# The first MLP split 6 and 10 instead of 8 and 8 around the attention, and two-source additions of 1e-9

## The chip, the core and the metric

The kernel runs on one core of a Trainium2 chip. A core has five engines with a queue of instructions each: TensorE (PE: matmuls, with PEld for the weight load ahead of each), VectorE (DVE), ScalarE (ACT), GpSimd (POOL) and SyncE (SP, which here issues nearly all DMAs). Each engine takes its own queue in order, and the engines wait for each other through semaphores. The metric is the device time of one execution in microseconds, the median of the runs.

## What is computed

Four batches of 576 positions go through block-causal attention with 8 heads of 64, then through two MLPs of 512 x 2048 x 512 on all 2304 rows, the second with a rational function instead of a squared ReLU.

```python
scores = scale * np.matmul(q, k.transpose(0, 1, 3, 2))
scores = np.where(block_i >= block_j, scores, -1000000000.0)   # blocks of 64
attn = np.exp(scores - np.max(scores, axis=-1, keepdims=True))
attn = attn / (np.sum(attn, axis=-1, keepdims=True) + 1e-09)
x = np.matmul(attn, v)                # 2304 x 512 after the heads are joined
h = np.maximum(x @ w_in, 0.0)         # first MLP, 2048 inner units
x = h * h @ w_out
h = x @ w_in2                         # second MLP
g = (a0 + a1*h + a2*h*h + a3*h*h*h) / (1 + |b0|*|h| + |b1|*h*h + 1e-6)
out = g @ w_out2
```

## The kernel before

Every MLP product is made three times with operands split into a high part in fp32r and the rest, `PAIRS`: high by high, low by high, high by low. The 2048 inner units of an MLP are 16 slices of 128. A slice has one tile of `w_in` (kind `i`) and one of `w_out` (kind `o`).

**The stages.** There are three.

- Attention with part A of the first MLP. The loop over `i` walks 128 slots; a slot is one group of score rows of one head (`GROUPS`). Heads 0 to 7 are visited twice with two slots each (slots 0 to 31), all later heads once with four slots. Heads below 10 (`PLAIN`) run in plain fp32, the others in split fp32r; slot 40 is the first of head 10. In slot `i` the scores of `i` are made (`emit_s`, PE), their maximum (`emit_max`, DVE, L342) and exponential (`emit_exp`, ACT, L355), the division of slot `i-1` is prepared (`emit_norm`, DVE and POOL; L367 and L378 add the 1e-9), and the transposes of slot `i-3` and the product with `v` of slot `i-4` follow on PE. Between them `advance` takes steps of `moe_a`, which is part A: 8 of the 16 slices, for one batch at a time, in two pieces of 320 and 256 columns (`SUBS`). A step is 3 matmuls. For each piece there is an h part (8 slices x 4 steps; each slice ends in `relu_square`, with two ACT operations, one on DVE, L526, and one on POOL, L527) and a y part (4 x 8 steps, with a copy by ACT each). Its sums go to DRAM (`yp`). `steps` sets how many steps a slot gets: one from slot 20 (`FIRST`) to 36 (`WIDE`), then as many that batch 0 ends at slot 68 (`SECOND`), then 4. Batches 0 to 2 run beside the attention; batch 3 runs behind it.
- Part B: the other 8 slices on all 2304 columns, in blocks of 384, 384, 512, 512 and 512 (`blocks2`), 40 units of 24 matmuls (lines 722 and 762), added to `yp`.
- The second MLP (part C) in blocks of 512, 512, 512, 384, 384, 80 units (lines 722 and 831).

**The weights** come packed and are converted on the chip by `Converter`: a 512 KB DMA into a raw buffer (3 buffers until part B, then 2), one ACT operation (L117), four DVE operations (L118, L119, L121, L122), and one call later the split, ACT (L110) and POOL (L111). `convA` converts the 16 tiles of part A in the attention, one call whenever `due(i)` steps up: at slots 3, 6, 9, 13, 16, 19, then 21, 23 and so on to 39, and 41. `convB` converts 12 tiles of part B beside batch 3's part A, one call per 9 steps, and the first three calls may move up to slot 64 (`gate_b`). `conv3`, one call per unit of part B, converts the rest of part B's tiles, then half of part C's into DRAM (`waiting`), then the other half. The tiles in `waiting` are loaded in B's last block and split by `split_late` (L714, L715), one per unit, into the first units of part C.

**Order.** The code above is the program's order, and a scheduler of the framework then sets the order in which each engine's queue holds the instructions.

## Time and profile before

| | us |
|---|---|
| median of 3 runs (1019.84 to 1020.8) | 1020.14 |
| the profiled execution | 1019.09 |
| its span, first to last instruction | 1016.9 |
| PE busy | 995.2 (98%) |
| PEld busy | 882.0 (87%) |
| DVE busy | 733.4 (72%) |
| ACT busy | 722.5 (71%) |
| POOL busy | 582.0 (57%) |

The profiled execution is 1.05 us under the median, and 2.2 us of it lie outside the span. A matmul's recorded duration overlaps that of the next, so PE counts as busy also where its matmuls are spaced out; the spacing of starts tells more. PEld is idle where matmuls come slowly: its share is 53 to 75% in the first 100 us and close to 100% from 200 to 400 us. The granted clock is 1.000, the 2.4 GHz level, in the whole span.

### The profile page before, as it was taken

What the parts mean: (1) busy time and instruction counts of PE and PEld (TensorE: products, weight loads), DVE (VectorE), ACT (ScalarE), POOL (GpSimd) and SP (SyncE); (2) the same over time, 40 slices, a digit from 0 to 9 for tenths busy, and PEclk for the clock granted to TensorE, in tenths of its full rate; (3) what the DMA queues carried; (4) which work ended last, traced back from release to release, by engine and by line L of the source; (5) the groups of instructions that cost most, each with busy time, mean ns of one, the idle gap of its engine ahead of it and who ended that gap; (6) DMA issues with size and microseconds to landing.
All of it is one profiled execution on the core that took longest, in us unless ns stands there. A gap on an engine that the chain in (4) does not pass through costs nothing. (4 is left out here: it accounts for less than half of the span.)

```text
span 1016.9 us, 16852 instructions
## 1 busy us (share of the span) xinstructions
PE 995.2 (98%) x5721; PEld 882.0 (87%) x5721; DVE 733.4 (72%) x1344; ACT 722.5 (71%) x1526; POOL 582.0 (57%) x632
## 2 busy tenths in 40 slices
PE   7999998999999999999999999999999999999997
PEld 5677998999999999999888888887888888899996
DVE  6899588868767646776667756887766766777766
ACT  7779687768777746564555557887787776787775
POOL 4677686868676745530132448767556554655552
PEclk9999999999999999999999999999999999999999
DMA  9766335233332204557656572001101100100000
GB/s 284 243 198 213 120 99 154 90 120 110 116 93 81 72 31 148 176 197 253 227 166 199 182 239 81 1 1 42 43 1 32 42 1 1 56 18 1 32 1 31
DMA packets 63892, 106.57 MB, mean 105 GB/s; under 512 B 16064, under 2 KB 34496, under 8 KB 63808
## 3 DMA queue, kind: packets, MB, share of 16 engines
q1 hardware_dynamic: 63520, 105.34, 32.3%
q8 instruction: 45, 0.74, 0.3%
q14 instruction: 39, 0.32, 0.1%
q10 hardware_dynamic: 288, 0.16, 0.1%
HBM read 79.17 MB, written 23.07 MB: 101 GB/s over the span
## 5 line engine op out<-in xcount | busy, mean ns | idle before, releaser
L831 PE MATMUL yc<-w_co,gc 128*128 128x512 f32 x864 | 211.8, 391 | 3.1 <-ACT gc L791 3.1
L722 PE MATMUL hc<-xc,w_ci 128*128 128x512 f32 (+1 forms) x960 | 211.2, 368 | 0.0
L722 PEld LDWEIGHTS hc<-xc,w_ci 128*128 128x128 f32 x960 | 176.1, 188 | 26.3
L831 PEld LDWEIGHTS yc<-w_co,gc 128*128 128x128 f32 x864 | 161.1, 188 | 36.0 <-ACT gc L791 4.6
L792 POOL TENSOR_TENSOR gc<-t,gc 128x512 fp32r<-128x512 f32 (+1 forms) x78 | 104.7, 1349 | 126.5 <-issue 103.6
L497 PE MATMUL ha<-xt,w_ai 128*128 128x320 f32 (+1 forms) x768 | 121.5, 304 | 0.1
L510 PE MATMUL ya<-ga,w_ao 128*128 128x320 f32 (+1 forms) x768 | 116.8, 299 | 3.3 <-ACT r L523 1.3
L817 POOL TENSOR_TENSOR wq<-wq,ab 128x512 f32<-128x512 f32 (+1 forms) x78 | 96.3, 1234 | 28.7 <-ACT wq L815 28.5
L497 PEld LDWEIGHTS ha<-xt,w_ai 128*128 128x128 f32 x768 | 107.5, 189 | 4.7 <-issue 3.0
L510 PEld LDWEIGHTS ya<-ga,w_ao 128*128 128x128 f32 x768 | 106.4, 189 | 5.1 <-ACT r L523 1.5
L762 PE MATMUL yb<-gb,w_bo 128*128 128x512 f32 (+1 forms) x480 | 105.8, 368 | 0.1
L722 PE MATMUL hb<-xb,w_bi 128*128 128x512 f32 (+1 forms) x480 | 105.8, 368 | 0.1
L791 ACT ACTIVATE gc<-t 128x512 fp32r<-128x512 f32 (+1 forms) x80 | 47.1, 589 | 72.9 <-DVE t L800 72.9
L818 DVE TENSOR_TENSOR t<-hc,t 128x512 f32<-128x512 f32 (+1 forms) x80 | 51.0, 637 | 66.1 <-ACT t L816 66.1
L762 PEld LDWEIGHTS yb<-gb,w_bo 128*128 128x128 f32 x480 | 87.6, 188 | 12.0 <-issue 0.5
L722 PEld LDWEIGHTS hb<-xb,w_bi 128*128 128x128 f32 x480 | 87.4, 188 | 11.6 <-ACT yo L515 0.5
L383 POOL TENSOR_SCALAR p<-p,stat 64x64 f32<-64x64 f32 (+4 forms) x110 | 63.2, 575 | 50.8 <-DVE stat L379 14.6
L418 DVE TENSOR_TENSOR pt<-tp,pt 128x512 fp32r<-128x512 f32 (+3 forms) x110 | 59.2, 540 | 28.2 <-ACT pt L417 25.9
L798 DVE SCALAR_TENSOR_TENSOR wq<-wq,ab 128x512 f32<-128x512 f32 (+1 forms) x80 | 55.4, 692 | 33.5 <-ACT ab L797 23.0
L400 PE MATMUL tp<-ident,p 128*128 128x128 f32 x480 | 77.7, 278 | 0.4 <-DVE xp L453 0.2
L417 ACT ACTIVATE pt<-tp 128x512 fp32r<-128x512 f32 (+3 forms) x110 | 52.8, 481 | 27.2 <-PE tp L400 25.7
L800 DVE SCALAR_TENSOR_TENSOR t<-t,coef,ab 128x512 f32<-128x512 f32 (+1 forms) x80 | 66.9, 836 | 1.7
(137 smaller groups left out, 1987.7 us busy)
## 6 DMA issues: line engine op xcount, KB each, us to landing
kr<-in_k_dram SPq DMA_DIRECT2D x32, 288.0 KB, 3.6
raw_ci<-in_wi_dram SPq DMA_DIRECT2D x16, 512.0 KB, 4.2
raw_co<-in_wo_dram SPq DMA_DIRECT2D x16, 512.0 KB, 4.4
qr<-in_q_dram SPq DMA_DIRECT2D x24, 320.0 KB, 3.3
raw_ai<-in_wi_dram SPq DMA_DIRECT2D x8, 512.0 KB, 5.9
raw_ao<-in_wo_dram SPq DMA_DIRECT2D x8, 512.0 KB, 4.1
raw_bi<-in_wi_dram SPq DMA_DIRECT2D x8, 512.0 KB, 3.5
raw_bo<-in_wo_dram SPq DMA_DIRECT2D x8, 512.0 KB, 3.5
```

The lines of the kernel that those rows point to most:

```text
L383: nc.gpsimd.tensor_scalar(pv, pv, st[r:P, 6 + n:7 + n], 0.0, op0=ALU.mult, op1=ALU.add)
L400: nc.tensor.transpose(ps[:, at:at + P], ptile(slots[i][0], t)[:, P * c:P * (c + 1)], ident)
L418: nc.vector.tensor_tensor(low, src, f(high), op=ALU.subtract)
L497: nc.tensor.matmul(ps[:, 0:n], w[:, zw, P * kk:P * (kk + 1)], xt[:, zx, kk, first:end], start=i == 0, stop=i == 3 * KK - 1)
L510: nc.tensor.matmul(ps[:, 0:n], wA["o", m][:, zw, P * c:P * (c + 1)], gs[m][:, zg, 0:n], start=i == 0, stop=i == 3 * HALF - 1)
L722: nc.tensor.matmul(ps[:, 0:n], w[:, zw, P * kk:P * (kk + 1)], xt[:, zx, kk, 0:n], start=i == 0, stop=i == 3 * KK - 1)
L762: nc.tensor.matmul(acc[j, c][:, 0:n], wB["o", m][:, zw, P * c:P * (c + 1)], g[:, zg, 0:n], start=m == 0 and i == 0, stop=last and i == 2)
L792: (nc.vector if u - 2 >= len(units) - END else nc.gpsimd).tensor_tensor(g[:, 1, 0:n], t, f(g[:, 0, 0:n]), op=ALU.subtract)
L798: nc.vector.scalar_tensor_tensor(w, w, Q0, r, op0=ALU.add, op1=ALU.mult)
L800: nc.vector.scalar_tensor_tensor(t, t, a0, r, op0=ALU.add, op1=ALU.mult)
L817: (nc.vector if u >= len(units) - END else nc.gpsimd).tensor_tensor(w, w, ab, op=ALU.mult)
L831: last = nc.tensor.matmul(acc[j, c], g[:, zg, P * c:P * (c + 1)], w3["o", m][:, zw, :], start=m == 0 and i == 0, stop=m == NM - 1 and i == 2)
```

## The change

- Part A takes 6 slices (`MA`), part B 10 (`MB`). `STEPS`, the steps of a batch, goes from 128 to 96: 2.5 steps per slot from slot 36 to 68 instead of 3.5, then 3 instead of 4. Part B has 50 units instead of 40.
- `convA` has 12 tiles instead of 16, and `due` one rate of 0.33: calls at slots 3, 6, 9 and so on to 39.
- `convB` still converts 12 tiles, but one per 7 steps instead of 9. `conv3` has 8 tiles of part B instead of 4 in an order of its own, then 20 tiles for `waiting` instead of 16, then 12 instead of 16.
- The two additions of 1e-9 (L367, L378) become `scalar_tensor_tensor`: (x + 1e-9) max x, with x as both sources.

```diff
-HALF = NM // 2
+MA = 6
+MB = NM - MA
...
-                nc.vector.tensor_scalar(sm[:, 1, :, t0:t1], sm[:, 0, :, t0:t1], 1e-9, None, op0=ALU.add)
+                raw = sm[:, 0, :, t0:t1]
+                nc.vector.scalar_tensor_tensor(sm[:, 1, :, t0:t1], raw, 1e-9, raw, op0=ALU.add, op1=ALU.max)
...
-        nc.vector.tensor_scalar(st[:, 4:4 + n], st[:, 2:2 + n], 1e-9, None, op0=ALU.add)
+        nc.vector.scalar_tensor_tensor(st[:, 4:4 + n], st[:, 2:2 + n], 1e-9, st[:, 2:2 + n], op0=ALU.add, op1=ALU.max)
...
-            for m in range(HALF):
+            for m in range(MA):
...
-    R1, R2, RS = 0.3, 0.5, 20
+    RATE = 0.33
 
     def due(i):
-        return int(i * R1) if i < RS else int(RS * R1 + (i - RS) * R2)
+        return int(i * RATE)
...
-    STEPS = 16 * HALF
+    STEPS = 16 * MA
...
-        return int(STEPS + 4 * (x - SECOND))
+        return int(STEPS + (x - SECOND) * STEPS / PER_B)
...
-    jobsB = [(f"b{kind}{m}", src[HALF + m], w2, kind, wB, m, nc.gpsimd)
-             for m in range(HALF) for kind, src in (("i", wi1), ("o", wo1))]
+    orderB = [(kind, m) for m in range(NB // 2) for kind in "io"] + [
+        ("i", 6), ("i", 7), ("i", 8), ("o", 6), ("i", 9), ("o", 7), ("o", 8), ("o", 9)]
+    jobsB = [(f"b{kind}{m}", {"i": wi1, "o": wo1}[kind][MA + m], w2, kind, wB, m, nc.gpsimd) for kind, m in orderB]
...
-    SPLITS = (73, 80, 87, 94)
+    SPLITS = (55, 60, 65, 70)
...
-        if n % 9 == 0:
-            convB(*(gate_b if n < 27 else paced))
+        if n % 7 == 0:
+            convB(*(gate_b if n < 21 else paced))
...
-    late = [(kind, m) for m in range(HALF, NM) for kind in "io"]
+    late = [(kind, m) for m in range(MA, NM) for kind in "io"]
...
-    units = [(j, m) for j in range(len(blocks2)) for m in range(HALF)]
+    units = [(j, m) for j in range(len(blocks2)) for m in range(MB)]
...
-        if u < 3 or u in (4, 6) or u > 6:
+        if u != 5:
             conv3(*done)
```

The scheduler's order shows the change at three places. First DVE's queue in slots 25 to 28, before: `raw_ao` and `cv_ao` are conversions of a weight tile, `stat` maxima of the scores, `s_0_1` is of part A.

```order
L342 TENSOR_REDUCE stat_124<-sx_738 128x1
L118 TENSOR_SCALAR raw_ao_585<-raw_ao_585 128x512
L119 SCALAR_TENSOR_TENSOR raw_ao_585<-raw_ao_585 128x512
L342 TENSOR_REDUCE stat_125<-sy_765 128x1
L121 TENSOR_SCALAR cv_ao_757<-cv_ao_757 128x512
L122 SCALAR_TENSOR_TENSOR cv_ao_757<-cv_ao_757,raw_ao_585 128x512
L342 TENSOR_REDUCE stat_126<-sx_782 128x1
L118 TENSOR_SCALAR raw_ao_639<-raw_ao_639 128x512
L526 SCALAR_TENSOR_TENSOR s_0_1_818<-ha_0_1_733,r_0_1_817 128x320
L342 TENSOR_REDUCE stat_127<-sy_835 128x1
L119 SCALAR_TENSOR_TENSOR raw_ao_639<-raw_ao_639 128x512
```

The same place in DVE's queue now:

```order
L344 TENSOR_REDUCE stat_124<-sx_738 128x1
L123 TENSOR_SCALAR cv_ao_730<-cv_ao_730 128x512
L124 SCALAR_TENSOR_TENSOR cv_ao_730<-cv_ao_730,raw_ao_499 128x512
L344 TENSOR_REDUCE stat_125<-sy_754 128x1
L344 TENSOR_REDUCE stat_126<-sx_771 128x1
L120 TENSOR_SCALAR raw_ao_552<-raw_ao_552 128x512
L529 SCALAR_TENSOR_TENSOR s_0_1_807<-ha_0_1_722,r_0_1_806 128x320
L121 SCALAR_TENSOR_TENSOR raw_ao_552<-raw_ao_552 128x512
L370 SCALAR_TENSOR_TENSOR sums_139<-sums_139 128x2x2
```

Two maxima now follow each other without a conversion's operations between them, and the addition to the sums is the new form (L370).

Second PE's queue over some slots of the fp32r heads, before: `sy` and `sx` are scores, `tp` transposes, `pv` products with `v`, `ha` part A's h part.

```order
L321 MATMUL sy_2543<-kk_2311,qh_2310 128x448
L321 MATMUL sy_2543<-k_two_1116,q_two_1115 128x448
L497 MATMUL ha_0_2_2550<-xt_1315,w_ai_435 128x320 x12
L457 MATMUL pv_0_2506<-pt_1409,vs_2394 128x320
L457 MATMUL pv_0_2506<-pt_1409,vs_2394 128x256
L457 MATMUL pv_0_2506<-pt_1409,vs_2394 128x128
L400 MATMUL tp_0_2516<-ident,p_1_98 128x128 x4
```

And now:

```order
L323 MATMUL sy_2358<-kk_2148,qh_2147 128x448
L323 MATMUL sy_2358<-k_two_1078,q_two_1077 128x448
L500 MATMUL ha_0_1_2344<-xt_1240,w_ai_346 128x320 x6
L500 MATMUL ha_0_2_2390<-xt_1240,w_ai_420 128x320 x3
L460 MATMUL pv_0_2327<-pt_1325,vs_2225 128x320
L460 MATMUL pv_0_2327<-pt_1325,vs_2225 128x256
L460 MATMUL pv_0_2327<-pt_1325,vs_2225 128x128
```

A slot holds 9 matmuls of part A instead of 12.

Third ACT's queue at the end of batch 3's second h part, before: `w_bo`, `w_bi` and `cv` are conversions for part B, `r`, `ga` and `s` part A's `relu_square`.

```order
L110 ACTIVATE w_bo_5751<-cv_bo_5695 128x512
L117 ACTIVATE cv_bi_5754<-raw_bi_5598 128x512
L523 ACTIVATE r_1_5_5772<-ha_1_5_5747 128x256
L524 ACTIVATE ga_1_5_5771<-r_1_5_5772 128x256
L525 ACTIVATE s_1_5_5773<-r_1_5_5772 128x256
L523 ACTIVATE r_1_6_5794<-ha_1_6_5778 128x256
L524 ACTIVATE ga_1_6_5793<-r_1_6_5794 128x256
L525 ACTIVATE s_1_6_5795<-r_1_6_5794 128x256
L110 ACTIVATE w_bi_5807<-cv_bi_5754 128x512
```

And now, at the last slice (`ga_1_5`) and the y part behind it:

```order
L112 ACTIVATE w_bo_5242<-cv_bo_5195 128x512
L527 ACTIVATE ga_1_5_5281<-r_1_5_5282 128x256
L528 ACTIVATE s_1_5_5283<-r_1_5_5282 128x256
L663 ACTIVATE xb_5421<-xb_5421 128x384 x3
L112 ACTIVATE w_bi_5292<-cv_bi_5245 128x512
L119 ACTIVATE cv_bo_5295<-raw_bo_5158 128x512
L518 ACTIVATE yo_1_0_5318<-ya_1_0_5288 128x256
L112 ACTIVATE w_bo_5328<-cv_bo_5295 128x512
```

The same conversion (`w_bo`, the fourth `o` tile of part B) stood ahead of slice 5 of 8 and now stands ahead of slice 5 of 6, the last.

## Rows read from the trace of the kernel before

**Rows 1.** The page's busy times, us, share of the span, instructions.

```profile
PE 995.2 (98%) x5721; PEld 882.0 (87%) x5721; DVE 733.4 (72%) x1344; ACT 722.5 (71%) x1526; POOL 582.0 (57%) x632
```

**Rows 2.** Stretches: length, PE, PEld, DVE, ACT, POOL busy us (count), clock, DMA share, GB/s.

```profile
38.20:93.20 55.00, 54.54 (x338) 40.70 (x337) 51.91 (x86) 46.44 (x115) 35.38 (x43) 1.00 0.68 207
93.20:112.00 18.80, 17.54 (x121) 14.44 (x121) 13.43 (x30) 12.22 (x33) 15.99 (x20) 1.00 0.57 187
...
186.90:328.00 141.10, 141.10 (x1106) 140.69 (x1104) 101.84 (x280) 109.17 (x294) 103.78 (x148) 1.00 0.34 102
225.00:250.00 25.00, 25.00 (x210) 24.94 (x210) 20.85 (x56) 21.56 (x59) 20.66 (x30) 1.00 0.38 108
358.00:415.10 57.10, 55.05 (x411) 54.23 (x410) 35.99 (x47) 32.49 (x75) 35.18 (x34) 1.00 0.30 103
```

**Rows 3.** Timeline of PE, 38 to 98 us: start, us, instructions, count.

```profile
40.64 0.95 PE L497 MATMUL ha<-xt,w_ai 128*128 128x320 f32 x3
...
92.86 0.28 PE L321 MATMUL sy<-kk,qh 128*128 128x64 f32 x1
```

**Rows 4.** Timeline of DVE, 69 to 79 us: start, us, instructions, count.

```profile
72.23 1.24 DVE L367 TENSOR_SCALAR sums<-sums 128x4 f32<-128x4 f32 x1
73.50 0.18 DVE L368 RECIPROCAL sums<-sums 128x4 f32<-128x4 f32 x1
```

**Rows 5.** DVE by line, 38.2 to 93.2 us: count | busy us, mean ns | idle.

```profile
L121 DVE TENSOR_SCALAR cv_ao<-cv_ao 128x512 f32<-128x512 f32 x7 | 7.7, 1095 | 1.0 <-ACT cv_ao L117 1.0
L119 DVE SCALAR_TENSOR_TENSOR raw_ao<-raw_ao 128x512 uint32<-128x512 uint32 x7 | 6.3, 906 | 0.1
...
L122 DVE SCALAR_TENSOR_TENSOR cv_ao<-cv_ao,raw_ao 128x512 uint32<-128x512 uint32 x7 | 5.2, 749 | 0.2
L367 DVE TENSOR_SCALAR sums<-sums 128x4 f32<-128x4 f32 (+1 forms) x5 | 4.1, 813 | 0.0
...
L118 DVE TENSOR_SCALAR raw_ao<-raw_ao 128x512 uint32<-128x512 uint32 x7 | 3.1, 439 | 0.0
```

**Rows 6.** ACT by line in the same stretch.

```profile
L117 ACT ACTIVATE cv_ao<-raw_ao 128x512 f32<-128x512 f32 x7 | 4.7, 677 | 0.0
L110 ACT ACTIVATE w_ao<-cv_ao 128x512 fp32r<-128x512 f32 x6 | 3.8, 628 | 0.0
```

**Rows 7.** Timeline of PE, 374 to 430 us, with idle before and releaser.

```profile
374.94 14.24 PE L510 MATMUL ya<-ga,w_ao 128*128 128x320 f32 x96
389.02 11.68 PE L497 MATMUL ha<-xt,w_ai 128*128 128x256 f32 x96
400.54 1.96 PE L510 MATMUL ya<-ga,w_ao 128*128 128x256 f32 x15
403.83 1.89 PE L510 MATMUL ya<-ga,w_ao 128*128 128x256 f32 x11 [1.34 <-ACT r L523]
...
415.11 4.33 PE L722 MATMUL hb<-xb,w_bi 128*128 128x384 f32 x24
```

**Rows 8.** The chain that ended last, in order of time: start, us, what.

```profile
742.41 5.44 PE hc L722 x24
...
917.56 3.12 PE hc L722 x18
```

**Rows 9.** ACT by line, 186.9 to 328 us: part A's work.

```profile
L524 ACT ACTIVATE ga<-r 128x320 fp32r<-128x320 f32 (+1 forms) x25 | 11.3, 450 | 0.5
...
L523 ACT ACTIVATE r<-ha 128x320 f32<-128x320 f32 (+1 forms) x24 | 9.9, 413 | 6.6 <-PE ha L497 5.2 <-PE pv L457 0.9 <-PE sy L321 0.2
...
L515 ACT ACTIVATE yo<-ya 128x320 f32<-128x320 f32 (+1 forms) x12 | 5.0, 419 | 0.9 <-ACT p L355 0.9
```

**Rows 10.** Timeline of ACT behind the attention.

```profile
402.33 0.63 ACT L110 ACTIVATE w_bo<-cv_bo 128x512 fp32r<-128x512 f32 x1 [2.98 <-DVE cv_bo L122]
```

**Rows 11.** Timeline of DVE there: conversions of part B's weights.

```profile
378.41 0.68 DVE L122 SCALAR_TENSOR_TENSOR cv_bi<-cv_bi,raw_bi 128x512 uint32<-128x512 uint32 x1
...
382.71 1.21 DVE L118 TENSOR_SCALAR raw_bo<-raw_bo 128x512 uint32<-128x512 uint32 x1 [3.63 <-DMA raw_bo<-in_wo_dram]
...
417.91 0.69 DVE L122 SCALAR_TENSOR_TENSOR cv_bo<-cv_bo,raw_bo 128x512 uint32<-128x512 uint32 x1
```

**Rows 12.** Timeline of PE in part C, the longest wait there.

```profile
707.44 2.11 PE L831 MATMUL yc<-w_co,gc 128*128 128x512 f32 x8 [1.60 <-ACT gc L791]
```

More of the change, by code (lines that the diff above doesn't have):

```diff
@@ L64, in attention_moe_moe @@
     xs2 = dram.tile([P, KK, NT], F32, name="xs2")
-    waiting = dram.tile([NM, P, 512], F32, name="waiting")
+    waiting = dram.tile([2 * MB, P, 512], F32, name="waiting")
     ident = const.tile([P, P], F32, name="ident")
@@ L507, in moe_a @@
                 ps = bank(f"ya{b_}_{s}_{c}")
-                for i in range(3 * HALF):
+                for i in range(3 * MA):
                     m, (zw, zg) = i // 3, PAIRS[i % 3]
                     nc.tensor.matmul(ps[:, 0:n], wA["o", m][:, zw, P * c:P * (c + 1)], gs[m][:, zg, 0:n],
-                                     start=i == 0, stop=i == 3 * HALF - 1)
-                    if i % 3 == 2 and i < 3 * HALF - 1:
+                                     start=i == 0, stop=i == 3 * MA - 1)
+                    if i % 3 == 2 and i < 3 * MA - 1:
                         yield
@@ L538, in attention_moe_moe @@
         (f"a{kind}{m}", src[m], wpool, kind, wA, m, nc.gpsimd)
-        for kind, src in (("i", wi1), ("o", wo1)) for m in range(HALF)])
+        for kind, src in (("i", wi1), ("o", wo1)) for m in range(MA)])
     load_qk(units[0], nc.scalar)
@@ L752, in attention_moe_moe @@
             g = gs.pop(u - LAG)
-            last = m == HALF - 1
-            if m == HALF // 2:
+            last = m == MB - 1
+            if m == MB // 2:
                 for c in range(KK):
@@ L801, in attention_moe_moe @@
             gf[u - 1] = t
-        split_late(u + len(blocks2) * HALF + LAG - SPLIT_AT, done)
+        split_late(u + len(blocks2) * MB + LAG - SPLIT_AT, done)
         if u < len(units):
```

17 lines of the change are left out of this document (9 added, 8 removed).

## The prediction

> **What bounds the kernel now.** I read the page's busy times first, then the stretches, then the timelines of the stretches where an engine stands out. PE is busy 98% of the span [rows 1], but that alone says little, since recorded matmuls overlap; PEld shows where matmuls really follow each other. From 186.9 to 328 us, 12 heads of the attention, PEld is busy in 140.69 of 141.10 us, while DVE, ACT and POOL have 72 to 77% [rows 2]: PE bounds there, and DVE, ACT and POOL have room. It is the same in parts B and C, where whole units follow each other at 5.44 us per 24 matmuls [rows 8]. The early attention is different. From 38.2 us (slot 20, just ahead of part A's first matmuls at 40.64) to 93.2 us (slot 40, head 10's first scores at 92.86) [rows 3], PEld has 40.70 of 55.00 us, and DVE 51.91, which is 94% [rows 2]. So in these 55 us DVE is the bound, with ACT next (46.44), and PE's work there is partly free. In 93.2 to 112 us PEld still has only 77% [rows 2]. Behind the attention, where batch 3's part A runs beside the conversions, PE waits a few us for ACT [rows 7], which itself waits 2.98 us for a conversion on DVE [rows 10]. The frame of the sum is thus: work moved from a stretch where DVE is the bound to one where PE is the bound and DVE is free should pay; work of PE moved between stretches that PE bounds should not matter.
>
> **PE's work that moves.** Per slice and batch, part A makes 24 matmuls of 320 columns and 24 of 256. The starts give 14.08 us per 96 (389.02 less 374.94), 146.7 ns each, and 11.52 per 96 (400.54 less 389.02), 120.0 ns each [rows 7]. Two slices less in four batches: 8 x 24 x (146.7 + 120.0) = 51.2 us less. In part B a matmul of 512 columns takes 5.44/24 = 226.7 ns and one of 384 takes 3.12/18 = 173.3 ns [rows 8], taken from part C, whose shapes are the same. Two slices more: 2 x 24 x (3 x 226.7 + 2 x 173.3) = 49.3 us more. Four steps (12 matmuls, 1.8 us) of the 51.2 lie before slot 40, where PE isn't the bound, and count nothing. So 49.4 less and 49.3 more: **-0.1 us**. The split by itself gains nothing while PE bounds both places.
>
> **Conversions in slots 20 to 40.** Before, ten conversions fall here (three `ai`, seven `ao`), now six. One costs DVE 439 + 906 + 1095 + 749 ns = 3.19 us [rows 5] and ACT 677 + 628 = 1.31 us [rows 6]. Four less: DVE 51.9 - 12.8 = 39.1 us, ACT 46.4 - 5.2 = 41.2 us. ACT becomes the bound of the stretch. The lowest end is ACT without a gap, 41.2 us, a gain of 13.8. At the 94% that DVE reaches now it would be 43.7. But ACT's exponential waits for DVE's maximum and both would be loaded alike, so I take ACT at 89%, 46.5 us: **-8.5 us**. The other end is a stretch that gives back only a third of DVE's 12.8, -4. What hides the four conversions afterwards: part B, where conv3 makes them one per unit of 4.2 to 5.4 us against 3.2 us of DVE; if that cover were gone they would cost their 12.8 us there. In slots 40 to 46 (93.2 to 112 us) the backlog of DVE no longer reaches over: PEld's share there rises from 77% towards that of later slots, 4 us of open time of which I take **-1.5 us** (0 to -3). In slots 0 to 20 the count of conversions is the same, six; I take **-0.5 us** for the additions (0 to -1.5).
>
> **The additions.** In this stretch L367 takes 813 ns on average, five times [rows 5], once 1.24 us, and the reciprocal of the same tile right behind it 0.18 us [rows 4]. The new form isn't in the trace. From above it costs what the old one does, from below what the reciprocal does, so its five save 0 to 3.2 us of DVE. I take it near the reciprocal, as it is as small; but with ACT as the bound this adds nothing to the term above.
>
> **The attention with less filler, slots 40 to 132.** From slot 68 a slot has 9 matmuls of part A instead of 12. Per head (four slots) PE takes 141.1/12 = 11.76 us now, and 12 matmuls at 133.3 ns less, 10.16 us, if it stays the bound. ACT has 109.17/12 = 9.10 us per head [rows 2], less one slice's two operations (450 + 413 ns [rows 9]) every second head: 8.67, 85% of the new pace where it was 77%. In h parts of 256 columns it is tighter: ACT without part A has 9.10 - (11.3 + 9.9 + 5.0)/12 = 6.9 us per head [rows 9], plus three slices at 0.8 to 0.86, 9.4 us, against PE's 5.36 + 36 x 0.120 = 9.7 (5.36 being 11.76 less 48 x 133.3 ns): 97%. The busiest 25 us before had ACT at 86% [rows 2] with PE undisturbed. Five such and similar parts of about 20 us lie in slots 40 to 132. Nothing in the trace shows ACT above 90% for so long, so the cost is bounded by 0 and by 8 us (ACT limited to its 86%: 9.4/0.86 = 10.9 per head, 1.2 more than 9.7, in some seven heads). I take **+3 us**. POOL and DVE lose half a slice of part A per head as well and stay below ACT.
>
> **Behind the attention.** Batch 3's part A shrinks by 12.8 us (counted above), but the same 12 tiles are converted beside it. Ten of them were left when its y part began: L122 from 378.41 to 417.91, nine intervals of 4.39 us [rows 11]. DVE waits for raw tiles in it, 3.63 us once [rows 11]: with three raw buffers a load starts only when an older tile is converted. From the first y part to the end of batch 3, PE now needs 72 matmuls of 320 and 144 of 256 columns, 27.8 us, while the ten conversions need 10 x 3.2 = 32 us at DVE's price and 43.9 at the pace shown. What queues behind them: ACT's split of the fourth `o` tile, the sixth of the ten, now stands ahead of the last slice's `ga`, without which the last y part can't run through. The first tile was done 4.1 us into the y part (379.09 less 374.94), so the sixth comes at 4.1 + 5 x 3.2 = 20 to 4.1 + 5 x 4.39 = 26 us, and PE wants it after 72 x 0.1467 + 72 x 0.120 + 15 x 0.120 = 21 us. The same split was late before: the last y part lasted from 400.54 to 415.11, 14.6 us instead of 11.5, 1.34 of the 3.1 in one wait for ACT [rows 7, 10]. I take 5.6 us of waiting in place of 3.1, **+2.5 us**. From below it is 0. From above, if the ten tiles keep 4.39 us each, the last is split 43.7 us into the y part, ahead of part B's first unit on ACT, whose product follows 2.5 us later, at 46.2; PE would be there at 27.8 + 36 x 0.1733 = 34.0, 12.2 us late against 3.1: +9.1.
>
> **Part C.** Splitting of late tiles reaches unit 13 instead of 9, close to the block's end where PE waits up to 1.60 us [rows 12], 2.7 in all around 700 us: **+0.5 us** (-1 to +2).
>
> **Sum.** -0.1 - 8.5 - 1.5 - 0.5 + 3 + 2.5 + 0.5 = -4.6 us. The profiled execution has 1019.09, so 1014.5 by it; the median stood 1.05 above, so **1015.5 us**. About 0.2% (2 us) is what a measurement here tells from no change.
>
> **Rivals.**
> - *The attention starves* (the slower side). With a quarter less of part A in each slot, ACT can't keep its dependent chain (maximum, exponential, transposes' copies) going at the new pace. If it can be busy no more than 82%, a head takes 8.6/0.82 = 10.5 us instead of a mean of 9.9 over slots 40 to 132 (16 heads at 10.16, seven at 9.36 with 2.5 steps), 0.57 x 23 = 13.1 us in place of my 3: 1025.6 us. It decides from about 84%, where the 4.6 us are used up. For it: no row shows ACT above 86% over 25 us. Against it: at 86% PE had no gap at all. The Trainium skill, Perfetto Trace Analysis, section Optimization Strategy, advises interleaving regimes with different busiest engines; by it, taking PE work out of the attention would be a loss. The rows agree only as far as PE was never short of work from 187 to 328 us.
> - *Everything early is gained.* ACT runs without gaps in slots 20 to 40 (-13.8) and nothing starves or stalls anew: -0.1 - 13.8 - 1.5 - 0.5 + 0.5 = -15.4: 1004.7 us. For it: DVE did run at 94% and later without gaps, so a bound engine can. Against it: ACT's waits for maxima.
> - *The conversions behind the attention set the end.* +9.1 in place of +2.5: 1022.1 us, just no change. For it: the measured pace of 4.39 us. Against it: that pace was partly the nine steps between calls, some 3.6 us.
> - *The early stretch keeps its pace*, as its slots wait for each other (scores, maximum, exponential, one score bank each) and not for DVE's time: -1 in place of -8.5: 1023 us. Against it: DVE has next to no idle time there [rows 5]. In this case the change doesn't do what it says: work leaves the stretch and time doesn't.
>
> **How the numbers follow.** Forecast 0.50, everything early 0.17, conversions 0.13, starving 0.12, early pace kept 0.08. Faster by over 0.2% (under 1018.1): most of the forecast's (0.44) and all of the second, 0.61. Within 0.2%: 0.05 of the forecast, 0.08 of the conversions and 0.05 of the last two, 0.18. Slower: the rest, 0.21. Cases of the forecast alone lie from 1009 to 1021; leaving out 1 in 10 on either side of all cases, the range is 1006 to 1023.
>
> **What would show it.** Right: slots 20 to 40 in 46 us with DVE below 90%; a steady head in about 10.2 us with PEld still near 99%; part B 49 us longer without waits; a wait of some 6 us around the last y part of batch 3. Wrong: slots 20 to 40 at 50 us or more; PEld below 95% in the steady attention with PE's waits on ACT or POOL; a wait of PE at part B's first product; new waits in part C. L367's successor at 0.2 us or at 0.8 tells which bound of the additions holds.

## The result and the profile after

The changed kernel takes 1035.53 us (median, 1033.55 to 1036.38) against 1019.99 of the kernel before on the same chip: a ratio of 1.0148 (1.0135 to 1.016), 15.5 us slower. The prediction said 1015.5 (1006 to 1023) and faster. The profiled execution has 1034.79 us, its span 1033.0, and this is where the 16.1 us between the spans came from. The marks are the maximum on DVE of slots 20, 40, 68 and 124, then the first matmul of part B, the first of part C and the end. (The marks 38.2 and 93.2 of the prediction are the maxima of slots 19 and 39, so its slots 20 to 40 are one slot early; the stretch is as long, 55.0 us. By one mark in both kernels it reads as follows.)

| stretch | before | after | difference | PE's work by count of steps | left over |
|---|---|---|---|---|---|
| slots 0 to 20 | 41.24 | 40.43 | -0.81 | 0 | -0.8 |
| slots 20 to 40 | 55.01 | 51.41 | -3.60 | -1.8 (4 steps) | -1.8 |
| slots 40 to 68 | 80.83 | 72.73 | -8.10 | -11.2 (28 steps) | +3.1 |
| slots 68 to 124 | 163.02 | 146.58 | -16.44 | -22.4 (56 steps) | +6.0 |
| slot 124 to part B | 75.01 | 59.95 | -15.06 | -16.0 (40 steps) | +0.9 |
| part B | 195.54 | 253.41 | +57.87 | +49.3 | +8.6 |
| part C | 406.23 | 408.49 | +2.26 | 0 | +2.3 |

A step is 3 matmuls of 133.3 ns on average (146.7 in slots 20 to 40, where all have 320 columns). "Left over" is the difference less PE's work. The -0.8 of slots 0 to 20 says nothing: two later profiles with the same code there have 39.66 and 41.67 us. The rows behind the table, stretches of the trace: length, busy time and count of PE, PEld, DVE, ACT, POOL, granted clock, DMA share, GB/s. Before:

```profile
0.00:41.24 41.24, 35.03 (x176) 23.44 (x177) 28.57 (x77) 29.54 (x90) 23.75 (x61) 1.00 0.86 271
41.24:96.25 55.01, 54.55 (x337) 41.06 (x335) 52.53 (x85) 46.75 (x117) 37.52 (x46) 1.00 0.68 209
96.25:177.08 80.83, 77.11 (x602) 73.48 (x601) 61.38 (x161) 59.65 (x161) 56.07 (x79) 1.00 0.43 128
177.08:340.10 163.02, 161.65 (x1266) 160.86 (x1267) 120.33 (x328) 124.71 (x338) 120.08 (x171) 1.00 0.33 99
340.10:415.11 75.01, 72.96 (x561) 72.11 (x561) 46.41 (x75) 44.01 (x108) 46.86 (x51) 1.00 0.29 98
415.11:610.65 195.54, 195.27 (x951) 172.37 (x949) 130.71 (x203) 111.61 (x203) 61.12 (x44) 1.00 0.63 207
610.65:1016.88 406.23, 398.68 (x1837) 338.71 (x1835) 293.42 (x419) 306.24 (x515) 236.63 (x184) 1.00 0.07 23
```

And after:

```profile
0.00:40.43 40.43, 34.51 (x176) 23.21 (x177) 29.76 (x79) 29.67 (x90) 26.05 (x62) 1.00 0.89 283
40.43:91.84 51.41, 50.90 (x324) 39.45 (x323) 38.55 (x70) 42.00 (x107) 28.89 (x41) 1.00 0.60 181
91.84:164.57 72.73, 67.49 (x518) 62.52 (x518) 55.17 (x152) 55.57 (x153) 50.33 (x75) 1.00 0.46 136
164.57:311.15 146.58, 142.88 (x1105) 139.47 (x1104) 123.23 (x323) 120.11 (x325) 113.71 (x165) 1.00 0.38 112
311.15:371.10 59.95, 57.42 (x439) 56.31 (x438) 35.58 (x66) 38.02 (x93) 38.03 (x43) 1.00 0.34 109
371.10:624.51 253.41, 247.43 (x1191) 218.78 (x1189) 153.76 (x235) 132.28 (x245) 68.18 (x51) 0.99 0.54 180
624.51:1033.00 408.49, 400.16 (x1837) 339.89 (x1835) 295.10 (x418) 306.84 (x515) 238.77 (x185) 0.99 0.07 23
```

The page's busy times after, which answer to [rows 1]:

```profile
PE 1000.8 (97%) x5577; PEld 879.6 (85%) x5577; DVE 731.2 (71%) x1340; ACT 724.5 (70%) x1522; POOL 564.0 (55%) x616
```

They tell little: PE has 5.6 us more in 144 recorded matmuls less. In the stretches two things stand out. In slots 68 to 124 PEld falls from 98.7% of the stretch to 95.1%, and a head takes 10.47 us (146.58/14) where 10.04 would have been PE's (11.64 less 12 x 0.1333). And part B, where PE was busy in 195.27 of 195.54 us, now has 6 us in which it isn't, and a granted clock below 1.

Most of the loss in part B has one place. The chain that ended last, in order of time, around part B's first block (start, us, what):

```profile
369.96 3.81 DMA raw_bo<-in_wo_dram
...
373.80 0.70 DVE raw_bo L120
374.49 1.70 DVE cv_bo L124
...
376.21 0.02 ACT w_bo L112
...
376.75 0.39 ACT yo L518 x2
377.14 1.66 DMA yp<-yo
...
378.91 0.39 ACT yo L518
...
379.35 5.49 PE hb L726 x16
```

The same on ACT's timeline (start, us, instruction, count, idle before and its releaser):

```profile
371.02 0.37 ACT L518 ACTIVATE yo<-ya 128x256 f32<-128x256 f32 x1
376.21 0.63 ACT L112 ACTIVATE w_bo<-cv_bo 128x512 fp32r<-128x512 f32 x1 [4.83 <-DVE cv_bo L124]
```

ACT stands 4.83 us at the split of a converted tile (`w_bo`), and behind it in ACT's queue are the copies `yo` out of the last PSUM banks of part A. PE, which has run part B's first two units from 371.10, wants these banks for its third and waits 3.89 us. (The last of the copies also waits for its output buffer, behind a DMA of 1.66 us.) The tile itself is late by its whole line: its load could start only at 369.96, when an older tile of the three in flight was converted. And once PE had waited, it came back at half the clock. PE's stretches there:

```profile
375.40:379.30 3.90, 0.06 (x1) 0.00 (x0) 2.57 (x4) 2.12 (x6) 1.50 (x2) 0.90 0.19 67
379.30:384.60 5.30, 5.25 (x16) 5.25 (x17) 2.61 (x5) 4.47 (x10) 2.98 (x2) 0.50 0.67 220
```

Behind 3.9 us with one matmul the granted clock is 0.50, the 1.2 GHz level, for the next 16 matmuls. They take 5.28 us (379.35 to 384.63), 330 ns each instead of 173.3: 2.5 us on top of the 3.9. That is 6.4 of part B's 8.6 us. PE's longest waits behind the attention, whole rest of the run (waited for: us in total, times, longest):

```profile
PE hb L726 <- ACT yo L518: 3.9, 1, 3.9
PE yc L835 <- ACT gc L795: 3.7, 3, 2.2
PE yb L766 <- DVE yp L771: 2.1, 2, 1.1
```

The third, the additions of `yp` at a block's end, is most of the rest of part B; why PE waits there now isn't shown. The second is the wait of [rows 12], 3.1 us in all before. Behind its longest, 2.18 us where before had 1.60, the clock fell again. PE's timeline there, and a stretch as above:

```profile
720.04 7.24 PE L835 MATMUL yc<-w_co,gc 128*128 128x512 f32 x24 [2.18 <-ACT gc L795]
```

```profile
719.80:723.30 3.50, 3.26 (x8) 2.58 (x9) 3.39 (x5) 2.90 (x6) 3.04 (x2) 0.51 0.00 0
```

The next matmul starts at 727.12: 24 matmuls take 7.08 us, at 226.7 ns each they would take 5.44. With 0.6 us more of waiting these 1.6 us are nearly all of part C's 2.3.

### The profile page after: what moved, and what is told of

Its sections match the earlier page's. It is cut to its first block, busy times and chain, and to the rows that moved or that the text cites. A ratio compares the mean times of both kernels' runs of the same rounds, so it can differ in the third digit from the quotient of the medians.

```text
span 1033.0 us, 16566 instructions
## 1 busy us (share of the span) xinstructions
PE 1000.8 (97%) x5577; PEld 879.6 (85%) x5577; DVE 731.2 (71%) x1340; ACT 724.5 (70%) x1522; POOL 564.0 (55%) x616
## 4 chain that ended last, share of the span: by engine, by line
PE 73%; DVE 10%; ACT 6%; DMA 6%; POOL 3%; issue 2%; SPq 0%; ACTq 0%; DVEq 0%; POOLq 0%
PE yc L835 15%; PE hc L726 15%; PE yb L766 9%; PE hb L726 9%; PE ha L500 5%; PE ya L513 5%; PE tp L403 4%; PE pv L460 3%; PE sx L323 3%; PE sy L323 3%; DMA raw_ci<-in_wi_dram 2%; PE pv L447 2%; DMA raw_bo<-in_wo_dram 2%; DVE t L804 1%; DVE ab L803 1%
## 5 line engine op out<-in xcount | busy, mean ns | idle before, releaser
L726 PE MATMUL hb<-xb,w_bi 128*128 128x512 f32 (+1 forms) x600 | 134.3, 373 | 3.9 <-ACT yo L518 3.9
L766 PE MATMUL yb<-gb,w_bo 128*128 128x512 f32 (+1 forms) x600 | 132.2, 368 | 2.1 <-DVE yp L771 2.1
L726 PEld LDWEIGHTS hb<-xb,w_bi 128*128 128x128 f32 x600 | 111.6, 191 | 18.1 <-ACT yo L518 4.2
L766 PEld LDWEIGHTS yb<-gb,w_bo 128*128 128x128 f32 x600 | 109.9, 189 | 16.9 <-ACT sb L528 1.5
L500 PE MATMUL ha<-xt,w_ai 128*128 128x320 f32 (+1 forms) x576 | 94.3, 306 | 0.0
L513 PE MATMUL ya<-ga,w_ao 128*128 128x320 f32 (+1 forms) x576 | 88.0, 298 | 2.5 <-ACT ga L527 1.9
L500 PEld LDWEIGHTS ha<-xt,w_ai 128*128 128x128 f32 x576 | 81.5, 189 | 4.5 <-issue 3.0
L513 PEld LDWEIGHTS ya<-ga,w_ao 128*128 128x128 f32 x576 | 80.4, 189 | 3.5 <-ACT ga L527 2.3
L530 DVE TENSOR_TENSOR gb<-sb,gb 128x512 fp32r<-128x512 f32 (+1 forms) x50 | 33.5, 669 | 69.0 <-ACT sb L528 68.9
L664 POOL TENSOR_TENSOR xb<-xb 128x512 fp32r<-128x512 f32 (+1 forms) x20 | 26.4, 1334 | 87.6 <-ACT xb L663 87.6
```

Of the source, the lines that this page charges most:

```text
L500: nc.tensor.matmul(ps[:, 0:n], w[:, zw, P * kk:P * (kk + 1)], xt[:, zx, kk, first:end], start=i == 0, stop=i == 3 * KK - 1)
L513: nc.tensor.matmul(ps[:, 0:n], wA["o", m][:, zw, P * c:P * (c + 1)], gs[m][:, zg, 0:n], start=i == 0, stop=i == 3 * MA - 1)
L726: nc.tensor.matmul(ps[:, 0:n], w[:, zw, P * kk:P * (kk + 1)], xt[:, zx, kk, 0:n], start=i == 0, stop=i == 3 * KK - 1)
L766: nc.tensor.matmul(acc[j, c][:, 0:n], wB["o", m][:, zw, P * c:P * (c + 1)], g[:, zg, 0:n], start=m == 0 and i == 0, stop=last and i == 2)
```

## The experiments

**The additions alone, and everything but the additions.** The first run is the kernel before with the two-source form, the second the changed kernel with the old form.

```diff
-        nc.vector.tensor_scalar(st[:, 4:4 + n], st[:, 2:2 + n], 1e-9, None, op0=ALU.add)
+        nc.vector.scalar_tensor_tensor(st[:, 4:4 + n], st[:, 2:2 + n], 1e-9, st[:, 2:2 + n], op0=ALU.add, op1=ALU.max)
```

> The kernel before (8 and 8 slices) with only the two additions of 1e-9 in their two-source form. In the profile of after, 88 of the small additions in the fp32r heads take 25.5 us where the old form took 18.9, and the long ones end within 20 ns of the end of a POOL instruction. Theory ports (a two-source addition waits for POOL's running instruction and lengthens the chain exponential, addition, division on POOL, transposes): 2 to 6 us slower than before, lost in slots 40 to 124, where 243.8 us become 246 to 250. Theory filler (the attention of after lost its pace for want of part A's matmuls, the additions do nothing): within 1 us of before, the stretch within 1 us of 243.8.

> The changed kernel (6 and 10 slices) with the two additions of 1e-9 in their old one-source form. Theory ports: slots 40 to 124, 219.3 us in after, come down by 4 to 7 us towards the 210.2 that the removed matmuls alone would leave (243.8 less 33.6), and the whole run by as much, to 1028 to 1031. Theory filler: the stretch stays within 1 us of 219.3 and the run within 1 us of 1035.5.

Measured: 0.9995 (0.9981 to 1.0009) of before for the first, 1035.37 us and 1.0136 (1.0116 to 1.0156) for the second, against 1.0148 for the whole change. The additions are not why the change lost; the theory of the ports, as an explanation of the total, falls. The mechanism is there all the same. DVE by line (count | busy us, mean ns | idle before), the additions in the fp32r heads between slots 68 and 124, before, in the first run, after and in the second run:

```profile
L378 DVE TENSOR_SCALAR stat<-stat 128x1 f32<-128x1 f32 (+1 forms) x56 | 11.3, 203 | 2.4 <-ACT p L355 2.1
```

```profile
L378 DVE SCALAR_TENSOR_TENSOR stat<-stat 128x1 f32<-128x1 f32 (+1 forms) x56 | 21.2, 379 | 2.4 <-ACT p L355 2.1
```

```profile
L381 DVE SCALAR_TENSOR_TENSOR stat<-stat 128x1 f32<-128x1 f32 (+1 forms) x56 | 18.1, 323 | 4.8 <-ACT p L357 4.1
```

```profile
L381 DVE TENSOR_SCALAR stat<-stat 128x1 f32<-128x1 f32 (+1 forms) x57 | 10.5, 184 | 5.5 <-ACT p L357 4.8
```

The two-source form takes 140 to 180 ns more on average. Where PE has 12 matmuls of part A per slot this changed nothing (163.03 us in slots 68 to 124 against 163.02). Where it has 9, the old form made these slots 2.4 us shorter (144.21 against 146.58), while slots 40 to 68 were 1.2 us longer (73.88 against 72.73): 1.2 us less in both together, where the theory of the ports had 4 to 7. Slots 40 to 68, 68 to 124 and part B of the second run:

```profile
94.06:167.94 73.88, 68.05 (x520) 62.80 (x519) 55.13 (x153) 56.30 (x155) 51.12 (x75) 1.00 0.46 137
167.94:312.15 144.21, 141.55 (x1100) 139.08 (x1101) 114.92 (x322) 119.16 (x323) 112.86 (x164) 1.00 0.39 112
372.17:622.98 250.81, 246.13 (x1190) 217.58 (x1189) 154.42 (x235) 132.10 (x245) 68.00 (x51) 0.99 0.56 182
```

**The conversions behind the attention.** The changed kernel with 10 instead of 12 tiles converted ahead of part B, the other 10 in the order of their use.

```diff
-NB = 12
+NB = 10
...
-        ("i", 6), ("i", 7), ("i", 8), ("o", 6), ("i", 9), ("o", 7), ("o", 8), ("o", 9)]
+        ("i", 5), ("i", 6), ("o", 5), ("i", 7), ("o", 6), ("i", 8), ("o", 7), ("i", 9), ("o", 8), ("o", 9)]
...
-        if u != 5:
-            conv3(*done)
+        conv3(*done)
```

> The changed kernel with 10 instead of 12 tiles of part B converted ahead of part B, the other 10 one per unit in the order in which they fall due. In after the last of the 12 is split at 381.1 us, PE waits 3.9 us at part B's first block, and runs the next 16 matmuls in 5.3 us at a granted clock of 0.50. Theory conversions (what stands ahead of part B's first products is the chain of conversions behind the attention, 4.2 us each, that cannot be shorter than the stretch left for it): both go, 6 to 8 us faster, 1027.5 to 1029.5 us, granted clock 1.000 throughout. Rival (DVE is loaded anyway, the wait moves to the first units of part B whose tiles come later): no more than 2 us faster, with new waits of PE in 380 to 420 us.

Measured: 1029.4 us, 1.0082 (1.0058 to 1.0105), so 6.1 us less than after's 1035.53 and 6.0 less than the run above, which was on the same chip. Part B is 249.16 us, 4.25 less; its wait for `yp` is still there (2.2 us). PE's timeline at part B's first block:

```profile
370.43 4.36 PE L726 MATMUL hb<-xb,w_bi 128*128 128x384 f32 x24
375.65 2.71 PE L726 MATMUL hb<-xb,w_bi 128*128 128x384 f32 x14 [0.86 <-ACT yo L518]
378.20 2.24 PE L766 MATMUL yb<-gb,w_bo 128*128 128x384 f32 x12
```

The wait is 0.86 instead of 3.89 us, and the 14 matmuls behind it go at full clock (2.55 us to the next group, 182 ns each). The two tiles less were what stood ahead of part B. New waits in part B stay small (0.4 and 0.3 us), so the rival doesn't hold.

**Filling the slots again.** The changed kernel, with one matmul more in every step of batches 1 and 2.

```diff
-                    nc.tensor.matmul(ps[:, 0:n], w[:, zw, P * kk:P * (kk + 1)], xt[:, zx, kk, first:end],
-                                     start=i == 0, stop=i == 3 * KK - 1)
+                    for again in range(2 if i % 3 == 0 and b_ in (1, 2) else 1):
+                        nc.tensor.matmul(ps[:, 0:n], w[:, zw, P * kk:P * (kk + 1)], xt[:, zx, kk, first:end],
+                                         start=i + again == 0, stop=i == 3 * KK - 1)
```

and the same in the y part.

> The changed kernel, where in batches 1 and 2 each step of part A makes its first product twice, 4 matmuls instead of 3, so that a slot from 68 on has 12 matmuls of part A again, as in the kernel before (the output is then not the reference's). That is 56 x 3 x 133.3 ns = 22.4 us more of PE in slots 68 to 124, which took 146.6 us in after and 163.0 before. Theory filler (with 9 matmuls per slot PE waits for the dependent chain of the attention, which 12 cover): the added 22.4 us cost only 16 to 18, 162.5 to 164.5 us. Rival (after's attention is longer for another reason, such as the order in the queues or the two-source additions): the full 22 or more, 168.5 us or over.

Slots 68 to 124 of this run:

```profile
165.82:328.51 162.69, 162.21 (x1273) 161.47 (x1271) 125.44 (x323) 120.10 (x325) 117.11 (x166) 1.00 0.35 102
```

22.4 us of matmuls more cost 16.1 us (162.69 less 146.58), and PEld is back at 99%. So 6.3 us of the changed kernel's slots 68 to 124 are waits that three matmuls per slot had covered: the 6.0 us left over in the table. This kernel was executed once, and both it and the changed kernel have the two-source additions.

**The split in the middle.** 7 and 9 slices, with the old additions.

```diff
-MA = 6
+MA = 7
...
-    RATE = 0.33
+    RATE = 0.37
...
-        if n % 7 == 0:
+        if n % 8 == 0:
```

> The split in the middle, 7 slices of part A and 9 of part B, with one-source additions, 12 tiles converted ahead of part B, 14 by the attention at a rate of 0.37. Slots 68 to 124 have 10.5 matmuls of part A each. If what the change costs were spread evenly, the run would stand halfway between 1020 and 1035.4, at 1027.7. Theory filler and conversions (both are covers that run out): nearly all is lost in the second step, since the conversions behind the attention need some 43 us and are left 49 at 8 slices, 43 at 7 and 37 at 6: 1020 to 1024.5 us, no wait of over 2 us at part B's first block. Rival (each slice moved costs alike): 1026 us or more.

Measured: 1024.04 us, 1.0017 (0.9999 to 1.0035). Stretches, slots 40 to 68, 68 to 124 and part B:

```profile
97.41:175.45 78.04, 74.15 (x570) 69.06 (x568) 57.01 (x156) 58.45 (x159) 53.35 (x77) 1.00 0.43 127
175.45:328.85 153.40, 151.35 (x1184) 150.18 (x1185) 120.77 (x325) 123.03 (x331) 118.15 (x168) 1.00 0.36 105
...
396.37:615.59 219.22, 219.22 (x1071) 194.31 (x1069) 139.13 (x217) 123.97 (x226) 67.15 (x49) 1.00 0.59 196
```

The first slice moved loses 2.8 us in slots 40 to 68 (78.04 against 80.83 less 5.6), 1.6 in slots 68 to 124 (153.40 against 163.02 less 11.2) and nothing in part B, where PE is busy throughout. The 6 and 10 split with the same old additions loses 4.3, 3.6 and 6.0 us in these places (73.88, 144.21 and 250.81), so the second slice adds 1.5, 2.0 and 6.0. The attention's loss thus begins with the first slice; only the cover of the conversions behind it runs out between 7 and 6 slices. The other 2.4 us of the changed kernel's 6.0 in slots 68 to 124 come with the two-source additions.

**What sets slots 20 to 40.** Six kernels, all made from the kernel before. First, the conversions called from slot 20 on without three of their four DVE operations:

```diff
-                nc.scalar.activation(c, high.bitcast(F32), AF.Abs, scale=65536.0)
+                nc.scalar.activation(c, high.bitcast(F32), AF.Abs, scale=1e-9 if light else 65536.0)
...
-                nc.vector.scalar_tensor_tensor(
-                    low, high, 0x80000000, low, op0=ALU.bitwise_and, op1=ALU.bitwise_or)
+                if not light:
+                    nc.vector.scalar_tensor_tensor(
+                        low, high, 0x80000000, low, op0=ALU.bitwise_and, op1=ALU.bitwise_or)
...
+        convA.light = i >= 20
```

> The kernel before, where the ten conversions called from slot 20 on leave out three of their four DVE operations (906 + 1095 + 749 ns each; the output is then not the reference's). That takes 27.5 us of DVE's 52.6 out of slots 20 to 40. The prediction's frame (DVE bounds these slots): the stretch from the maximum of slot 20 to that of slot 40, 55.1 us, comes down to ACT's 46.8 or a little more, 47 to 49 us. Theory PE (plain fp32 matmuls are recorded twice, at 242 ns for 288 columns, longer than the weight load ahead of them, so PE is dense there though PEld has 75%): the stretch stays at 53 us or more.

```profile
42.12:98.28 56.16, 53.86 (x322) 40.17 (x321) 27.84 (x59) 45.57 (x114) 33.37 (x46) 0.97 0.68 208
```

DVE is busy in 27.84 instead of 52.53 us, and the stretch isn't shorter. The clock was 0.97 in this one: 3.4 us of it were at half the clock (90.83 to 94.24), which is worth 1.7, so some 54.5 without. DVE alone doesn't bound it. (This kernel and the last three of the six were executed once each: 1025.65, 1020.01, 1018.68 and 1017.86 us, against 1021.8, 1020.88, 1018.4 and 1018.4 for the kernel before on the same chips.) Next, part A begun at slot 36:

```diff
-    FIRST, WIDE, SECOND = PER_B // 2 + MOE_AT, PER_B + MOE_AT, 2 * PER_B + MOE_AT
+    FIRST, WIDE, SECOND = PER_B + MOE_AT, PER_B + MOE_AT, 2 * PER_B + MOE_AT
```

> The kernel before with part A begun at slot 36 instead of 20: the 16 steps (48 matmuls) of slots 20 to 36 move into slots 36 to 68, which get 4 steps each instead of 3.5. Theory PE (PE bounds slots 20 to 40, and slots 40 to 68 have waits that more of part A can fill): slots 20 to 40 lose 6 to 9 us, slots 40 to 68 gain 4 to 6, the run is 1 to 3 us faster. Theory of the prediction (DVE bounds slots 20 to 40, PE's work is free there): slots 20 to 40 keep 54 us or more, slots 40 to 68 gain 6.4, the run is 5 to 6 us slower.

Slots 20 to 40 and 40 to 68:

```profile
43.01:97.12 54.11, 48.81 (x294) 33.73 (x291) 51.94 (x85) 45.66 (x112) 35.73 (x44) 1.00 0.72 227
97.12:183.38 86.26, 83.06 (x646) 79.95 (x644) 63.71 (x162) 62.36 (x166) 58.82 (x81) 1.00 0.41 120
```

14 steps less (6.2 us of PE) shorten the first by 0.9 us only and lengthen the second by 5.4, nearly all of what they are. The run is slower, 1.0034 (1.0021 to 1.0048). The theory of PE, with 6 to 9 us, missed. By this run alone the prediction's theory would stand (54 us or more in the one, nearly all of the steps' time paid in the other; it had the run 5 to 6 us slower, and it was 3.5), but the run before it shows that relieving DVE alone gains nothing. Slots 40 to 68 have no room for more of part A. The same kernel with 10 tiles ahead of part B as well:

```diff
-NB = 12
+NB = 10
...
+    orderB = [(kind, m) for m in range(NB // 2) for kind in "io"] + [
+        ("i", 5), ("i", 6), ("o", 5), ("i", 7), ("o", 6), ("o", 7)]
...
-        if u < 3 or u in (4, 6) or u > 6:
+        if u < 6 or u > 6:
```

> The kernel before with part A begun at slot 36, as in the run above, and with 10 instead of 12 tiles of part B converted ahead of part B, the other six one per unit in the order in which they fall due. Theory conversions: the waits of 2.8 us in batch 3's last part and at part B's first block (one of 1.34 for ACT) shrink by 1 to 2 us, with no new ones in part B: 1 to 2 us faster than the run above. Rival (the waits there come from the y part's own chain): no difference to the run above beyond 0.5 us.

Measured 1.0069 (1.0053 to 1.0085): not faster, but slower still, so both theories missed. From slot 124 to part B it took 76.1 us against 74.7: the wait for ACT became 1.89 us (0.9 in the run above), with 3.4 us at half the clock behind it. Part C took 2.1 us more (408.14 against 406.00); why isn't shown. At 8 slices taking two conversions away from ahead of part B gains nothing.

Next, the conversions from slot 20 on without ACT as well as without the three DVE operations:

```diff
-                nc.scalar.activation(c, high.bitcast(F32), AF.Abs, scale=65536.0)
+                if light:
+                    nc.vector.tensor_scalar(c, high.bitcast(F32), 1e-9, 0.0, op0=ALU.mult, op1=ALU.add)
```

and the rounded copy likewise.

> The kernel before, where from slot 20 on the conversions for part A use ACT no more: their two ACT operations (677 + 628 ns) become two short ones on DVE, and three of DVE's four operations are left out as in the earlier run that did only that (the output is then not the reference's). DVE stays under 40 of 55 us, ACT loses some 13 of 46.8 us in slots 20 to 40. Theory ACT (ACT's queue, in order and with the exponentials' waits in it, sets the pace of these slots: 0.85 of the stretch in before, 0.82 in after, 0.84 where part A's steps were taken out, and 56.2 us where DVE alone was relieved): the stretch from 55.0 to 45 to 49 us. Rival (the slots wait for each other, scores, maximum, exponential, transposes, whatever the conversions do): 53 us or more.

```profile
42.22:97.63 55.41, 54.46 (x340) 41.93 (x339) 46.03 (x80) 37.15 (x99) 37.48 (x47) 1.00 0.74 228
```

ACT has 37.15 instead of 46.75 us (DVE 46.03, since its replacements were longer than thought), and the stretch stays. The theory of ACT falls. Last, no conversions at all from slot 20 on, with part A as before and with part A begun at slot 36:

```diff
-        for kind, src in (("i", wi1), ("o", wo1)) for m in range(HALF)])
+        for kind, src in (("i", wi1), ("o", wo1)) for m in range(HALF)][:6])
...
-    wA = {}
+    class Reused(dict):
+        def __missing__(self, key):
+            return self["i", 0]
+
+    wA = Reused()
```

> The kernel before without the ten conversions called from slot 20 on, altogether: no DMA of the packed tile, nothing on ACT, DVE or POOL; part A uses the first converted tile in place of the ten missing ones (the output is then not the reference's). Taking DVE's share of them away (56.2 us) or DVE's and ACT's (55.4) left the 55.0 us of slots 20 to 40 as they were. Theory conversions (their DMAs of 512 KB and POOL's subtractions of 1.4 us, which were still there in those two runs, hold the slots up, and that is what the change saved with four conversions less): 46 to 50 us. Rival (the slots wait for each other, whatever runs beside them): 52.5 us or more.

> The kernel before without these ten conversions and with part A begun at slot 36 instead of 20: slots 20 to 36 hold the attention alone (the output is then not the reference's). Part A's steps taken out alone gave 54.1 us. Rival (the slots wait for each other): 50 us or more with nothing beside them. Theory of shares (PE's work of part A and the conversions each hide behind the other, so that only taking both away shows): 42 to 47 us.

Slots 20 to 40 of the one and of the other:

```profile
40.67:93.83 53.16, 52.15 (x330) 40.65 (x329) 26.21 (x51) 37.83 (x99) 24.16 (x39) 1.00 0.48 142
```

```profile
40.46:87.22 46.76, 46.23 (x293) 34.32 (x291) 23.27 (x49) 35.98 (x94) 21.29 (x37) 1.00 0.53 150
```

Without conversions 53.16 us, without part A 54.11, without both 46.76. The theory of shares holds: two loads of nearly the same length lie over each other, and taking one away shows the other. With the conversions gone, PE counts one for one: 14 steps less give 6.4 us less (14 x 3 x 146.7 ns are 6.2). PE's own floor for these slots was 53.2 us, and PEld was busy in only 40.65 of them, 76%. The changed kernel has four steps less there, 1.8 us, and four conversions less: 53.16 less 1.76 is 51.40, and it took 51.41. (That it meets the floor so exactly is luck: at 7 slices, with two steps and three conversions less, the same sum gives 52.28, and it took 53.06.)

Which engine carries the second load isn't shown. With part A taken out DVE had 51.94 of 54.11 us, so it may well be DVE there. Nor is it shown what of the conversions holds the stretch 1.9 us above PE's floor: without ACT's work for them and with DVE at 46.03 us it was 55.41, with DVE at 27.84 some 54.5. And without any conversions the whole run was no faster (1018.68 against 1018.4), as slots 68 to 124 took 1.6 us more, with 3.4 us at half the clock at their start.

**A version that beats both.** The kernel before, where POOL instead of ACT makes the rounded copy of a converted tile of part A, and the same with 7 slices in part A (the edit of the split in the middle, with two rates of conversions).

```diff
-                nc.scalar.activation(w[:, 0, :], c, AF.Copy)
+                if nm[0] == "a":
+                    eng.tensor_scalar(w[:, 0, :], c, 1.0, 0.0, op0=ALU.mult, op1=ALU.add)
+                else:
+                    nc.scalar.activation(w[:, 0, :], c, AF.Copy)
```

and for the second also

```diff
-    RATE = 0.33
+    R1, R2, RS = 0.3, 0.42, 20
```

> The kernel before, where the rounded copy of a converted weight for part A (628 ns on ACT, 16 times) is made by POOL, which then subtracts it as before. ACT loses 6.3 us of its 46.8 in slots 20 to 40 and some 4 us ahead of them; POOL gains some 9 us of its 37.6. Theory ACT: slots 20 to 40 become 3 to 5 us shorter, and the run 3 to 6 us faster than before, 1014 to 1017.5. Rival (slots wait for each other, or POOL, whose divisions stand in the same chain, becomes late): within 1.5 us of before or slower.

> 7 slices in part A and 9 in part B with one-source additions, as in the run of the split in the middle, with the rounded copies on POOL as in the run above and conversions in the attention at a rate of 0.3 until slot 20 and 0.42 then. Theory ACT: two conversions less in slots 20 to 40 are worth some 2 us on top of the run above and the thinner attention costs 1.6 us in slots 68 to 124, so it stands level with the run above, within 2 us. Rival (a slice moved to part B costs anyway): 3 us or more slower than the run above, as the middle split was against before.

Measured: 0.9964 (0.995 to 0.9979) of before for the first, 1016.91 us; 0.9995 (0.9979 to 1.0011) for the second, 3.3 us slower than the first, as its rival said. Two conversions less were worth nothing in its slots 20 to 40: 55.78 us, at a granted clock of 0.97. Slots 0 to 20, 20 to 40 and 40 to 68 of the first:

```profile
0.00:40.24 40.24, 34.50 (x178) 23.19 (x179) 28.48 (x78) 27.24 (x85) 29.33 (x67) 1.00 0.87 279
40.24:94.16 53.92, 53.18 (x334) 41.18 (x333) 50.87 (x85) 42.91 (x107) 45.74 (x55) 1.00 0.71 213
94.16:173.87 79.71, 77.24 (x603) 73.54 (x601) 59.84 (x160) 58.21 (x158) 56.69 (x80) 1.00 0.44 129
```

Each is 1.0 to 1.1 us shorter than before. In the first that says nothing, since profiles with before's code there have 40.46 to 43.01 us. In the second it is inside the 1.9 us that the floor of 53.16 leaves, and less than the 3 to 5 expected. Why it helps, where the run with still less of ACT's work showed nothing (55.41), isn't settled.

## Why the prediction was wrong, step by step

**The frame: DVE bounds slots 20 to 40.** This step failed, and with it the largest term. It rested on PEld's 40.70 of 55.00 us and DVE's 51.91 in [rows 2]: an engine at 94%, and PE open for a quarter of the time. DVE's 94% was true, but at half that load the stretch was as long. The change took from DVE and ACT what the sum said, 14.0 and 4.8 us (52.53 to 38.55 and 46.75 to 42.00; 12.8 and 5.2 were forecast), and the stretch gave 3.6. PE was open for 1.85 us (55.01 less 53.16), not for 14. In these slots plain fp32 matmuls take longer than the weight loads ahead of them (scores of 288 columns start 242 ns apart, their weight loads take 190), so PEld's share says little, and PE's 54.54 of 55.00 us in the same row, put aside as overlap, was nearer to the truth. The Trainium skill, Perfetto Trace Analysis, section Identifying the Most-Contended Engine, advises to judge TensorE's room by MFU (the multiplications made, as a share of the peak) and the weight loads' busy share; the frame went by the second alone. In the fp32r heads the runs agree with it (PEld at 98.7%, PE the bound), in the plain fp32 heads they don't (76%, PE the bound), and the measurement decides.

**Conversions, -8.5 us.** They gave -1.8, the distance to PE's floor. The four steps that "count nothing" gave their full 1.8. The rival that the early stretch keeps its pace had the size nearly right (-1 of time without the work), with a wrong reason: the slots don't wait for each other, as the 46.76 us without both loads show.

**PE's work moved, -0.1 us.** Right: -1.8, -33.6 and -16.0 against +49.3 nearly balance. But the places that lost matmuls didn't give their time back in full.

**The attention with less filler, +3, and slots 40 to 46, -1.5.** Together +1.5; measured +9.1 (3.1 in slots 40 to 68, 6.0 in 68 to 124). This is the first rival, "the attention starves": it reckoned 10.5 us per head with ACT at 82%, and slots 68 to 124 took 10.47 with ACT at 82% (120.11 of 146.58). Its 13.1 us for the whole were too much, the +3 too little. The refilled slots show that it is the missing matmuls. The additions have a part in it, against "of no effect elsewhere": with the old form the two places lost 4.3 and 3.6 us, 7.9 in all. That ACT alone is what can't keep up isn't shown: DVE has 84% there, and 6.8 us of its time come from the two-source additions (18.1 less 11.3). In slots 40 to 68 that was not tried by refilling; there the run with more of part A shows only that more fills nothing.

**Behind the attention, +2.5.** Here the upper bound of +9.1 had the mechanism nearly right. With 4.39 us per tile it put the last split 43.7 us into the y part and part B's first product of the second kind at 46.2. Measured: the y part began at 338.12, the last split at 381.07 (43.0 later), the product at 384.63 (46.5 later). The tiles came 3.9 us apart (345.02 to 380.34, nine intervals). The chain of conversions kept its length: before, the last split began 43.7 us after the start of the y part (418.64 less 374.94). What shrank is the stretch beside it, from the y part's start to part B: 40.2 us before (415.11 less 374.94), 33.0 now (371.10 less 338.12). By the bound's own reckoning PE was 11.7 us late at that product (46.5 less the 27.8 and 40 matmuls of 173.3 ns) instead of 3.1, so +8.6; 2.5 of them are the half clock, which the bound didn't have, so that its size was in part luck. I took the sixth tile in place of the last as what PE would wait for, and argued 4.39 down for the nine steps between calls. PE waited in fact not for the tile itself but for PSUM banks whose copies stood behind a tile's split in ACT's queue, at the next place down the line. The half clock behind the wait, 2.5 us, was in no term, nor were the 2.1 us of waits at the blocks' ends of part B.

**The additions, -0.5, of no effect elsewhere.** No effect on the total was right (0.9995). The price was not: five of L367's successor took 702 ns on average, against 813 before and the 180 taken, and the commoner one on `stat` got slower, 203 to 323 ns. The form had no part in the first: in the run of everything but the additions the old form took 699 ns, in the run of the additions alone the new one 805. For `stat` the bound from above, that the new form costs no more than the old, failed. DVE by line in slots 20 to 40 of after:

```profile
L370 DVE SCALAR_TENSOR_TENSOR sums<-sums 128x4 f32<-128x4 f32 (+1 forms) x5 | 3.5, 702 | 0.0
```

**Part C, +0.5.** Measured +2.3. The mechanism was the right one, the wait of [rows 12], which is 0.6 us longer in all; the 1.6 us of half clock behind it were in no term. The same is seen with 10 tiles (408.42). With the old additions the wait is as long (2.20 us), the clock stays, and part C is at 407.72; with 7 and 9 slices the longest wait is 1.0 us, and part C is at 405.74.
